# Two of the 48 paired dV stores of a cached-attention and SwiGLU backward kernel, issued in parts of 49, 49, 30 and of 49, 49, 25, 5 partitions

## The chip, the cores and the metric

The kernel runs on one core of one Trainium2 chip. The metric is the time of one execution on the device in microseconds (us).

## What is computed

The reference is one decode step of a transformer block and its gradients. Four batch rows `x` of 512 numbers pass a layer norm and attention over a key and a value cache of 32 heads of 4096 x 128 bf16 numbers for each batch row, and then a gated SwiGLU block. What is returned is the output and the gradients with respect to everything but `B_x`:

```python
def _A_ref(x, k_cache, v_cache, wq, wo):
    q = (x @ wq).reshape(B, Sq, H, Dh).transpose(0, 2, 1, 3)
    scores = jnp.einsum("bhqd,bhkd->bhqk", q, k_cache) * (Dh ** -0.5)
    p = _softmax(scores, axis=-1)
    o = jnp.einsum("bhqk,bhkd->bhqd", p, v_cache)
    return o.transpose(0, 2, 1, 3).reshape(B, Sq, H * Dh) @ wo
h = x + _A_ref(_layernorm(x), A_k_cache, A_v_cache, A_wq, A_wo)
h2 = h + _B_ref(_layernorm(h), B_w1, B_w3, B_w2)   # silu(x w1) * (x w3) @ w2
_out, _vjp = jax.vjp(_f, A_x, A_k_cache, A_v_cache, A_wq, A_wo, B_w1, B_w3, B_w2)
return (_out, *_vjp(grad_out))
```

There are 4 x 32 = 128 heads. For each, the caches K and V are 1 MB, and so are their gradients dK and dV. With one query a head, dV is an outer product of the probabilities with the head's row of dO, and dK one of dS with the row of q.

## The kernel before

All traffic between HBM and the on-chip memory goes through an `arena` of 23 slots, each 4160 bf16 columns on all 128 partitions; one head (4096 columns, 8 KB a partition) fills a slot, a pair of heads (8192 columns, 16 KB a partition) two neighbouring ones. The schedule is written out by hand: the program order on each engine is the order of the source, and all large transfers are issued by SyncE (SP), on one queue, in program order.

The forward pass loads K and V of each head (L178 and L186). The weights and V are then loaded again (V at L833 for single heads, L1280 for pairs), and the backward part stores dV (L817) and dK (L1255) of the first 32 heads one by one. The other 96 heads go as 48 pairs `t` = 0 to 47. For each pair:

- `load_pair` (L1280) brings 2 MB of V into a pair of slots, three pairs ahead of its use;
- `front_pair` transposes it on TensorE (L1298), copies it back on ScalarE (L1299) and multiplies (L1313);
- `grad_pair` is called once for dV (`out_3`, from `more_V`) and once for dK (`out_2`, from the loop over `t`). It takes a pair of slots (`Slot2`, the one that was given back longest ago), VectorE writes the outer product into it (`outer_pair`, L1379, 128 x 8192), and SP stores it (L1389): one DMA of 128 rows of 16 KB. `give()` hands the slots on; the next work that writes them waits until the store has landed.

```python
def two_heads(ap, t):
    b, h = t % B, H0 + t // B * 2
    return ap[b, h:h + 2].rearrange("h (p j) d -> (h p) (j d)", p=P // 2)
```

So a pair's 128 rows are 128 pieces of 16 KB that lie one after the other in HBM. `lead_V` lets the dV stores run ahead of the dK stores of the same pair by a few pairs, fewer towards the end. Between these, `side(s)` stores the gradients of the weights (L1072, L1119, L1135, L1146). The last eleven transfers of the program are stores of pairs (L1389).

SP has 530 transfers to issue. The program gives them eight completion semaphores in turn, and each transfer waits, besides for its data, until the one eight places before it has landed. In this order the dV store of pair 16 is number 416 (counted from 0), that of pair 34 number 482, and the last store of all is number 529.

Of the kernel before, what the change touches and what calls it, by code (L numbers as in the profile page):

```python
# [21 lines left out]
SP = 32  # L22
NPAIR = 8
OLD = 9


@with_exitstack
def kernel(
# [22 lines left out]
    nc = tc.nc  # L51
    P = nc.NUM_PARTITIONS
# [5 lines left out]
    Dh = A_k_cache.shape[3]  # L58
# [6 lines left out]
    SJ = Sk // P  # L65
# [50 lines left out]
    def age(i):  # L116
        return given["n"] - given.get(i, -NSLOT)
# [7 lines left out]
    class Slot:  # L125
        def __init__(self, name, src=free):
            self.i = src[0]
            if part["B"] and src is free:
                lone = sorted((i for i in free if i not in part["pairs"]), key=age, reverse=True)
                self.i = lone[0] if name in SIDE or lone and age(lone[0]) >= OLD else max(free, key=age)  # L130
            src.remove(self.i)
# [76 lines left out]
    for i in range(2):  # L208
        t = fcon.tile([P, 64], BF16, name=f"onesw{i}")
# [4 lines left out]
    def ones_window(col):  # L214
# [11 lines left out]
                          in_=rowg[:, None, :, None].to_broadcast([P, 4, 8, 4]))  # L226
# [738 lines left out]
    with ExitStack() as c2:  # L965
# [306 lines left out]
# [4 lines that stand above are left out]
        def load_pair():  # L1276
            t = npv["next"]
            npv["next"] += 1
            pV[t] = Slot2()
            nc.sync.dma_start(out=pV[t].t[:, 0:2 * SJ * Dh], in_=two_heads(A_v_cache, t))  # L1280

        def load_pairs(t):
            while npv["next"] < NT and (npv["next"] <= t or len(V2s) + 2 * len(pV) < 6 and len(Slot2.choices()) > 1
                                          and -min(Slot2.choices())[0] >= OLD - 2):
                load_pair()
# [92 lines left out]
        def outer_pair(dst, col2, row):  # L1378
            nc.vector.tensor_tensor(  # L1379
                out=dst.rearrange("p (j r t) -> p j r t", r=Dh // 2, t=2),  # L1380
                in0=col2[:, :, None, :].to_broadcast([P, 2 * SJ, Dh // 2, 2]),
                in1=row.rearrange("p (r t) -> p r t", t=2)[:, None, :, :].to_broadcast([P, 2 * SJ, Dh // 2, 2]),
                op=ALU.mult,
            )

        def grad_pair(out_ap, t, col2, row):
            g_ = Slot2()
            outer_pair(g_.t[:, 0:2 * SJ * Dh], col2, row)
            nc.sync.dma_start(out=two_heads(out_ap, t), in_=g_.t[:, 0:2 * SJ * Dh])  # L1389
            g_.give()  # L1390

        O0, S0, S1, L, LP = 2, 21, 35, 5, 3
# [2 lines left out]
        def more_V(upto):  # L1395
            while gvd["n"] < min(SP, upto):
                s = gvd["n"]
                P_pairs(s)
                replicate("rdo", s - s % REP)
                grad_V(s)  # L1400
                P_pairs(s + 1)
                P_pairs(s + 2)
                gvd["n"] += 1
                if s % REP == 2 and s + 2 < SP:
                    replicate("rdo", s + 2)
                elif s % REP == 2:
                    replicate_pair("rdo", 0)
                if s >= SP - 2:
                    P2_pair(s - SP + 2)
            while gvd["t"] < NT and SP + 2 * gvd["t"] + 2 <= upto:  # L1410
                t = gvd["t"]
                P2_pair(t)
                replicate_pair("rdo", t // B)
                grad_pair(out_3, t, pP2.pop(t), reps["rdo", "p", t // B][:, t % B, :])
                P2_pair(t + 1)
                gvd["t"] += 1
                if t % B == 2:
                    replicate_pair("rdo", t // B + 1)
# [57 lines left out]
        for t in range(NT):  # L1476
            s = SP + 2 * t
            load_pairs(t + LP)
            if t % B == 2:
                replicate_pair("rq", t // B + 1)  # L1480
            if t + LP < NT:
                front_pair(t + LP, lambda: side(s))
            else:
                if t + LP == NT:
                    rows_out()
                    rows_T()
                side(s)
            more_V(s + 2 + lead_V(s))
            grad_pair(out_2, t, pdS[t // 2][:, t % 2], reps["rq", "p", t // B][:, t % B, :])
            if t % 2 == 1 and t + 1 < NT:  # L1490
                group_dS_pair((t + 1) // 2)
            side(s + 1)
# [31 lines left out]
```

## Time and profile before

| | |
|---|---|
| Time, median of 3 runs | 1697.54 us (1696.87 to 1697.6) |
| Span of the profiled execution | 1696.2 us |
| Bytes read from HBM, written to it | 422.59 MB, 282.34 MB |
| Mean rate of the 16 DMA engines | 417 GB/s |
| Busy: TensorE matmul, VectorE, ScalarE, GpSimd | 73%, 73%, 57%, 20% |
| A pair's store (2048 KB), issue to landing, median | 27.9 us |
| A pair's load (2048 KB), issue to landing, median | 32.1 us |
| Outer product of a pair on VectorE (L1379) | 4.42 us |

The only time that the profiled execution has of its own is its span, from its first instruction to its last; the median of the runs is 1.3 us above it, for what lies around the span and for the scatter between executions.

How to read it: a line of the kernel is given as L and its number; SPq is SP's queue of DMA issues. "DMA" rows give the mean busy share of the 16 DMA engines of the core, so that one engine busy alone is 0.06 of them. In a list of waits, "A <- B: us, times, longest" says how long A stood still until B released it. Each DMA is carried out by several engines, and each of them reports its own part on the DMA's semaphore: the trace has sixteen such updates for every DMA of 128 rows, with their times.

### The profile page before, as it was taken

The numbers are of one execution on the slowest core, as the hardware profiler recorded it, in microseconds if no ns is written. First come the engines' busy times: TensorE is split into PE (matmuls) and PEld (weight loads), VectorE is DVE, ScalarE is ACT, GpSimd is POOL, SyncE is SP. The second block draws the span as 40 slices with busy tenths as digits, with TensorE's granted clock in tenths as the row PEclk, the third lists the DMA queues.
The fourth block names the chain that finished last, engine by engine and source line by source line (L and its number), as shares of the span: only waits on it lengthen the run. The fifth ranks groups of instructions, "written<-read, shape, count | busy, mean of one in ns | idle before, by whom it ended". The sixth has DMA issues, their size and how long they took to land.

```text
span 1696.2 us, 37839 instructions
## 1 busy us (share of the span) xinstructions
PE 1233.4 (73%) x16228; PEld 943.4 (56%) x16228; DVE 1234.4 (73%) x1198; ACT 959.5 (57%) x1490; POOL 336.9 (20%) x583
## 2 busy tenths in 40 slices
PE   5889888888888888877876755667665666766650
PEld 4777667666677666655655544444444444444440
DVE  5989999999998997667766466575665655655683
ACT  3555544454454544677665555666665666666650
POOL 1211222222222222222231121011210102011120
PEclk8999999999999999899898689886678777676675
DMA  9999999999999999999999999999999999999995
GB/s 401 424 424 424 424 424 424 424 424 423 416 423 406 424 414 397 395 414 425 425 425 429 428 429 428 429 430 429 429 429 428 418 430 429 422 418 425 415 429 230
DMA packets 81000, 707.45 MB, mean 417 GB/s; under 512 B 8748, under 2 KB 12984, under 8 KB 15296
## 3 DMA queue, kind: packets, MB, share of 16 engines
q1 hardware_dynamic: 80416, 704.94, 99.0%
q8 instruction: 127, 2.08, 0.5%
q14 instruction: 41, 0.34, 0.0%
q0 software_dynamic: 416, 0.10, 0.0%
HBM read 422.59 MB, written 282.34 MB: 416 GB/s over the span
## 4 chain that ended last, share of the span: by engine, by line
DMA 46%; DVE 9%; PE 3%; issue 2%; ACT 1%; DVEq 0%; POOL 0%; SPq 0%; ACTq 0%
DMA out_dram<-arena 43%; DVE arena L1379 7%; DMA arena<-in_A_v_cache_dram 3%; DVE arena L806 1%; PE M_ps L472 1%; DVE arena L457 1%; PE pt_w L601 0%; ACT arena L1299 0%; ACT Pn L436 0%; DVEq L1519 0%; PE kP_ps L482 0%; DVE dPr L1326 0%; PE pt_tps L1298 0%; PE gu_ps L873 0%; PE dn_ps L904 0%
## 5 line engine op out<-in xcount | busy, mean ns | idle before, releaser
L1299 ACT COPY arena<-pt_tps 128x1024 bf16<-128x1024 bf16 x384 | 369.8, 1023 | 232.3 <-PE pt_tps L1298 231.6
L1298 PE MATMUL pt_tps<-ident_b,arena 128*128 128x128 bf16 x3072 | 308.1, 272 | 204.7 <-DMA arena<-in_A_v_cache_dram 149.4
L1298 PEld LDWEIGHTS <-arena 128*128 128x128 bf16 x3072 | 263.9, 125 | 304.2 <-DMA arena<-in_A_v_cache_dram 172.8
L1379 DVE TENSOR_TENSOR arena<-arena 128x8192 bf16<-128x8192 bf16 x48 | 212.5, 4427 | 205.1 <-DMA out_dram<-arena 202.3
L472 PE MATMUL M_ps<-arena 128*128 128x130 bf16 x4096 | 285.1, 222 | 42.9 <-DMA arena<-in_A_v_cache_dram 42.2
L457 DVE TENSOR_TENSOR arena<-arena 128x4096 bf16<-128x4096 bf16 x128 | 292.5, 2285 | 23.9 <-POOL arena L453 23.9
L472 PEld LDWEIGHTS <-arena 128*128 128x128 bf16 x4096 | 251.9, 99 | 64.0 <-DMA arena<-in_A_v_cache_dram 57.2
L1379 DVE TENSOR_TENSOR arena<-dS,arena 128x8192 bf16<-128x8192 bf16 x48 | 212.3, 4424 | 73.0 <-DMA out_dram<-arena 73.0
L364 DVE STREAM_TRANSPOSE arena<-arena 128x512 f32<-128x512 f32 (+1 forms) x321 | 250.7, 797 | 0.0
L359 ACT COPY arena<-pt_tps 128x1024 bf16<-128x1024 bf16 x128 | 129.5, 1012 | 188.9 <-PE pt_tps L358 150.5
L1376 POOL COPY arena<-arena 128x128 bf16<-128x128 bf16 x48 | 55.3, 1153 | 492.3 <-ACT arena L1353 286.3
L370 POOL TENSOR_TENSOR W<-qrep,wmask 128x128 bf16<-128x128 bf16 x128 | 120.2, 939 | 85.6 <-PE S_ps L390 70.8
L801 ACT COPY arena<-pt_tps 128x1024 bf16<-128x1024 bf16 x128 | 121.7, 1025 | 26.1 <-PE pt_tps L800 24.8
L453 POOL COPY arena<-P_all 128x64 bf16<-128x64 bf16 x128 | 32.7, 255 | 412.8 <-ACT P_all L447 409.8
L806 DVE TENSOR_TENSOR arena<-dS,arena 128x4096 bf16<-128x4096 bf16 x32 | 73.2, 2293 | 35.0 <-DMA out_dram<-arena 34.7
L800 PE MATMUL pt_tps<-ident_b,arena 128*128 128x128 bf16 x1024 | 78.5, 229 | 27.1 <-ACT arena L801 27.1
L1313 PE MATMUL dP_ps<-arena 128*32 128x512 bf16 x768 | 85.7, 484 | 7.6 <-ACT arena L1299 7.3
L800 PEld LDWEIGHTS <-arena 128*128 128x128 bf16 x1024 | 67.2, 104 | 37.5 <-issue 35.9
L447 ACT COPY P_all<-pt_P 32x64 bf16<-32x64 bf16 x256 | 52.1, 204 | 53.6 <-PE pt_P L443 51.4
L806 DVE TENSOR_TENSOR arena<-P,arena 128x4096 bf16<-128x4096 bf16 x29 | 66.4, 2295 | 19.8 <-DMA out_dram<-arena 19.8
L358 PE MATMUL pt_tps<-ident_b,arena 128*128 128x128 bf16 x1024 | 80.1, 222 | 0.0
L482 PE MATMUL kP_ps<-arena,onesw 128*32 128x512 bf16 x1024 | 79.6, 388 | 0.0
(245 smaller groups left out, 1576.5 us busy)
## 6 DMA issues: line engine op xcount, KB each, us to landing
out_dram<-arena SPq DMA_DIRECT2D x96, 2048.0 KB, 27.9
arena<-in_A_v_cache_dram SPq DMA_DIRECT2D x160, 1024.0 KB, 15.9
arena<-in_A_k_cache_dram SPq DMA_DIRECT2D x128, 1024.0 KB, 15.3
arena<-in_A_v_cache_dram SPq DMA_DIRECT2D x48, 2048.0 KB, 32.1
out_dram<-arena SPq DMA_DIRECT2D x72, 1024.0 KB, 20.2
arena<-in_A_wq_dram SPq DMA_DIRECT2D x8, 1024.0 KB, 14.4
arena<-in_B_w_dram SPq DMA_DIRECT2D x8, 896.0 KB, 15.3
out_dram<-arena SPq DMA_DIRECT2D x6, 896.0 KB, 28.4
```

The costliest lines, as they stand in the source:

```text
L359: nc.scalar.copy(out=KT[:, c * GW:(c + 1) * GW, :], in_=pt[:])
L364: nc.vector.transpose(out=KT[:, c * w_:(c + n) * w_], in_=Kn[:, c * w_:(c + n) * w_])
L370: nc.gpsimd.tensor_tensor(out=W[:, hl], in0=qrep[:, :, s:s + 1].to_broadcast([P, 4, 32]), in1=wmask[:, hl, None, :].to_broadcast([P, 4, 32 ...
L457: nc.vector.tensor_tensor(out=PK[:, :, 0:Dh].rearrange("p j (r t) -> p j r t", t=2), in0=Ks[s].heads().rearrange("p j (r t) -> p j r t", t=2),
L472: nc.tensor.matmul(hold["M"][:], lhsT=Vn[:, j, :], rhs=PK[:, j, :], start=(j == 0), stop=(j == SJ - 1))
L800: nc.tensor.transpose(pt[:, i, :], v[:, g * GW + i, :], ident_b[:])
L801: nc.scalar.copy(out=v[:, g * GW:(g + 1) * GW, :], in_=pt[:])
L806: nc.vector.tensor_tensor(out=dst.rearrange("p j (r t) -> p j r t", t=2), in0=col2[:, :, None, :].to_broadcast([P, SJ, Dh // 2, 2]), in1=r ...
L1298: nc.tensor.transpose(pt[:, i, :], v[:, g * GW + i, :], ident_b[:])
L1299: nc.scalar.copy(out=v[:, g * GW:(g + 1) * GW, :], in_=pt[:])
L1313: nc.tensor.matmul(rows["acc"][32 * c:32 * (c + 1), :], lhsT=zt[t % B][:, 32 - m:64 - m], rhs=v[:, j0:j0 + 4, :], start=(pl == 0 and u == ...
L1379: nc.vector.tensor_tensor(out=dst.rearrange("p (j r t) -> p j r t", r=Dh // 2, t=2), in0=col2[:, :, None, :].to_broadcast([P, 2 * SJ, Dh / ...
```

## The change

The stores of dV for pairs 16 and 34 are issued as several DMAs, one behind the other, over consecutive partitions: 0 to 48, 49 to 97 and 98 to 127 for pair 16; 0 to 48, 49 to 97, 98 to 122 and 123 to 127 for pair 34. Every other transfer, all stores of dK among them, stays whole. The bytes, the slots and the order of all other work stay as they are.

```diff
+CUTS = {16: (49, 98), 34: (49, 98, 123)}
...
         def grad_pair(out_ap, t, col2, row):
             g_ = Slot2()
             outer_pair(g_.t[:, 0:2 * SJ * Dh], col2, row)
-            nc.sync.dma_start(out=two_heads(out_ap, t), in_=g_.t[:, 0:2 * SJ * Dh])
+            dst, src = two_heads(out_ap, t), g_.t[:, 0:2 * SJ * Dh]
+            cuts = (0, *CUTS.get(t, ()), P) if out_ap is out_3 else (0, P)
+            for p0, p1 in zip(cuts, cuts[1:]):
+                nc.sync.dma_start(out=dst[p0:p1, :], in_=src[p0:p1, :])
             g_.give()
```

SP then issues 535 transfers instead of 530, and each of the five that come in addition takes its turn among the eight semaphores. The next outer product that reuses the slots waits for all parts.

## The prediction

> **What bounds the kernel now.** I read the page's slices first, then the chain and the waits, then the windows of the last 25 us, and last the landing times of each DMA.
>
> ```profile
> DMA  9999999999999999999999999999999999999995
> DMA 46%; DVE 9%; PE 3%; issue 2%; ACT 1%; DVEq 0%; POOL 0%; SPq 0%; ACTq 0%
> q1 hardware_dynamic: 80416, 704.94, 99.0%
> q8 instruction: 127, 2.08, 0.5%
> ```
>
> The DMA engines are busy from the first slice to the last but one, and the chain that ended last is mostly DMA. So the work of the engines decides, not TensorE or VectorE (73% each). The last slice has a 5 where the others have 9. The windows (start and end, length, busy times, clock, DMA share, GB/s) show why:
>
> ```profile
> 1660.00:1670.00 10.00, 0.00 (x0) 0.00 (x0) 6.79 (x2) 0.00 (x0) 0.00 (x0) 0.50 1.01 429
> 1670.00:1676.00 6.00, 0.00 (x0) 0.00 (x0) 0.00 (x0) 0.00 (x0) 0.00 (x0) 0.50 0.86 369
> 1678.00:1686.00 8.00, 0.00 (x0) 0.00 (x0) 0.00 (x0) 0.00 (x0) 0.00 (x0) 0.50 0.07 29
> 1686.00:1694.00 8.00, 0.00 (x0) 0.00 (x0) 0.00 (x0) 0.00 (x0) 0.00 (x0) 0.50 0.06 27
> ```
>
> All compute is over, and from about 1677 to 1694.9 the DMA share is 0.06: one engine of sixteen, at 27 GB/s. The DMA view of the window from 1678 to 1696 has 31 packets, 0.44 MB:
>
> ```profile
> DMA packets 31, 0.44 MB, mean 25 GB/s; under 512 B 4, under 2 KB 4, under 8 KB 4
> ```
>
> Four are the 4-byte updates of four DMAs, 27 are rows of 16 KB, 607 ns from start to start. One engine still has the rest of four stores to write when the others have nothing left, and the program waits for it:
>
> ```profile
> SPq L1519 <- DMA out_dram<-arena: 27.6, 2, 22.8
> SPq L1389 <- DVE arena L1379: 564.8, 91, 12.1
> DVE arena L1379 <- DMA out_dram<-arena: 76.3, 18, 7.1
> ```
>
> (The third line is VectorE's waits from 1440 to 1676: the outer products wait for slots whose stores have not landed. SP, in the second, waits for those outer products.) The sixteen updates of a DMA, sorted, tell how far the engines are apart. Span times in us, of the first seven, the next eight and the last:
>
> ```
> DMA                       first seven      next eight       last
> 416 (dV, pair 16)      1156.4..1158.0   1161.4..1163.1    1171.2
> 482 (dV, pair 34)      1454.8..1455.4   1458.9..1460.4    1475.4
> 529 (the last store)   1674.6..1674.9   1676.6..1677.6    1694.9
> ```
>
> One engine trails: 9.8 us behind the middle at pair 16, 15.7 at pair 34, some 18 at the end, where the gap stops growing because new stores need slots that it must first free. From landing 416 to 529 each engine had 508.1 us of packets (836 rows of 16 KB or their worth at 607 ns, and an update of 6 ns for each DMA); the last needed 523.7 us, a factor 1.03. It was never without work, so each row costs it 0.607 x 1.03 = 0.625 us of the end. The early seven needed 517 to 518 us, so they stood for up to 9 us, 6 of them after 1356.
>
> **The change part by part.** *The whole store* gives each engine 8 rows: 128 rows, sixteen updates. *The parts* have 49, 30, 25 and 5 rows, and no DMA of the trace has such a count. Every DMA that it does have is dealt without remainder: 128 rows as 16 x 8, GpSimd's 4-row stores as 4 x 1. Dealt so over at most 16 engines, 49 rows go as 7 x 7, 30 as 15 x 2, 25 as 5 x 5, 5 as 5 x 1. If every deal begins at the same engine, the two stores together, 16 rows an engine before, become:
>
> ```
> engines      pair 16         pair 34            sum   against 16   us at 0.607
> first five   7+7+2 = 16      7+7+5+1 = 20       36       +20         +12.1
> next two     7+7+2 = 16      7+7     = 14       30       +14          +8.5
> next eight         2                  0          2       -14          -8.5
> last one           0                  0          0       -16          -9.7
> ```
>
> Which row holds the trailing engine? The two 4-row stores by GpSimd, near 1130 and 1263 us, put their 1 KB rows on four engines. Followed packet by packet to the next update, all four, both times, are among the early seven. So the engines at which a short deal begins are early, and the trailing engine isn't one of the first four. Seven early engines fit the first seven of the deal. Of the remaining nine places, eight give -14 rows and one -16; I take 14.
>
> [...]
>
> *The trailing engine* then ends 14 x 0.625 = 8.7 us earlier, at 1686.2 (10.0 and 1684.9 with 16 rows).
>
> *The first five* are late next. From 1156.4 to 1158.0 at DMA 416 they have 508.1 + 12.1 = 520.2 us of packets: 1676.6 to 1678.2 if they never stand, 1674.9 + 12.1 = 1687.0 if they stand as often as before. The second is above 1686.2, but with 8 rows more each from pair 16 on they lose the lead that made them stand; I take a value in between, and they don't decide. If the first five were of the middle eight, they would end at 1677.6 + 12.1 = 1689.7 at worst.
>
> *Five more DMAs on SP.* An issue is 0.33 us and issues of one burst start 0.44 us apart, so 5 x 0.44 = 2.2 us on a queue that stood 564.8 us at L1389; behind it only the dK store of the same turn and a V load three pairs ahead. Cost 0, or 2.2 us if that cover were gone. The nearest row for the tail of a small DMA is GpSimd's 4 KB store, 6.6 us to land, here beside other engines' work: also 0.
>
> *The semaphores.* With three or four parts in the turn of eight, a transfer behind pair 16 waits in effect for the one six places before it, behind pair 34 five places. Stores follow each other every 4.9 us and land 27.9 us after issue, 5.7 places. By the old landings, four issues behind pair 34 would wait: 483 (a dK store, 2.6 us), 484 (a weight's store, 7.3 us), 485 (a V load, 11.5 us) and 486 (5.4 us). The 14 - 8 = 6 rows that the trailing engine has lost at pair 16 take 3.8 us off each. What remains, up to 7.7 us on a load, is hidden: the load is needed three pairs (some 45 us) later, and the trailing engine has 15 us of other rows before it. The middle engines, which took 17.7 us from its issue to its landing, may stand for 3 us, and they have 8.5 us to spare. Cost 0; up to 7.7 us if that cover were gone.
>
> [...]
>
> **Sum.** 1696.2 - 8.7 = 1687.5 us of span; the median of the runs lies 1.3 us above the profile, so 1688.8 us.
>
> **The rivals.**
> 1. *The first five end last* (0.15). The standing of the early seven doesn't shrink, or the first five are engines of the middle eight. The end is 1687.0 to 1689.7 instead of 1694.9, the time 1689.6 to 1692.3. For it: the early seven's 9 us of standing. Against it: where 4-row stores go.
> 2. *Slower: the trailing engine is among the first seven* (0.08). Each row added to it moves the end by 0.625 us from the first one on: +20 rows give 1710.0 us, +14 give 1706.3. For it: no view gives its number; against it, the 4-row stores and the group of just seven early ones.
> 3. *No change* (0.04). Rows go by partition whatever the count, each engine keeps 8 of each store, and the change doesn't move what it seems to: 1697.5 us. A deal of ceil(49/16) = 4 rows an engine belongs here too if the trailing engine is among the first twelve: 4+4+2 and 4+4+2 rows or one more, +2.5 to 3.1 us at most; further back it would gain.
> 4. *Slower by the semaphores* (0.02). SP falls so far behind at pair 34 that the trailing engine itself stands. It decides from the point where SP stalls longer than its backlog, 15.7 - 3.8 = 11.9 us, against 7.7 us above. Price: some 5 us for a slot turn, with the rows' gain lost as well: about 1702.
>
> **Chances and range.** The forecast case has 0.71, rival 1 0.15: faster by over 0.2% (3.4 us, about what a measurement of this kernel can tell from no change) 0.86, within 0.2% 0.04, slower 0.10. The range takes 16 rows and 0.5 us of scatter at the low end (1687.5 - 0.7), and rival 1's worst at the upper: 1686.8 to 1692.4. Rivals 2 to 4, 0.14, are left out.
>
> **What would show it.** Right: the parts have 7, 7, 15, 7, 7, 5 and 5 data-carrying updates that come late and the others at once; the last slices still show one or a few engines, but for about 9 us less; from the DMAs behind pair 16 on the early seven land about where the middle eight do, and the last update comes 14 rows, some 8.6 us, nearer to them. The end is shared: near it five engines are busy (a share near 0.3) close to when the trailing one ends. Wrong: the old order of early, middle and last behind pair 16 (rival 3), a last update that trails more than before (rival 2), or a DMA share under 0.95 for tens of us behind pair 34 (rival 4).

## The result and the profile after

The changed kernel takes 1725.91 us in the median of 5 runs (1723.17 to 1727.47), the kernel before 1697.54 us. The ratio is 1.0164, 95% interval 1.0152 to 1.0176: 28.4 us slower, where 8.7 us faster was forecast. The profiled execution has a span of 1723.2 us against 1696.2.

The page of the kernel after: DMA share and rate in 40 slices of 43.1 us, DMA packets, and the first line of the queues.

```profile
DMA  9999999999999999999999999999999999899995
GB/s 401 424 424 424 424 424 424 424 424 423 418 421 412 424 411 397 381 425 424 426 426 428 429 428 428 430 419 372 409 413 409 411 429 424 319 408 424 414 412 231
DMA packets 81021, 707.45 MB, mean 411 GB/s; under 512 B 8769, under 2 KB 13005, under 8 KB 15317
...
q1 hardware_dynamic: 80437, 704.94, 98.4%
```

The GB/s row of the kernel before:

```profile
GB/s 401 424 424 424 424 424 424 424 424 423 416 423 406 424 414 397 395 414 425 425 425 429 428 429 428 429 430 429 429 429 428 418 430 429 422 418 425 415 429 230
```

The rate falls to 372 in the slice of pair 16 and to 319 in that of pair 34; in the four slices behind the first it is 409 to 413, where the kernel before has 418 to 429. Yet the share of busy time is a 9 in the first of these slices and an 8 in the second: the engines are mostly occupied and move less. The same bytes are moved, and SP's queue has 80437 packets instead of 80416. The 21 more are updates: two whole stores have 2 x 16, and the parts 7 + 7 + 15 + 7 + 7 + 5 + 5 = 53, as counted on the semaphores of the trace. So they go to as many engines as the prediction assumed.

The windows around the two stores say it more closely (the DMA share and GB/s are the last two columns). First before, then after:

```profile
1155.00:1175.00 20.00, 15.88 (x129) 10.51 (x128) 14.07 (x8) 14.93 (x19) 1.60 (x2) 0.59 1.01 428
1465.00:1485.00 20.00, 12.90 (x125) 7.86 (x121) 12.00 (x8) 13.50 (x19) 2.02 (x3) 0.83 1.01 421
```

```profile
1155.00:1175.00 20.00, 11.76 (x102) 7.58 (x101) 10.41 (x7) 11.26 (x15) 0.47 (x2) 0.67 1.00 369
1465.00:1485.00 20.00, 10.15 (x94) 6.79 (x90) 13.20 (x8) 10.90 (x15) 2.96 (x1) 0.72 0.77 245
```

From 1155 to 1175 the engines are fully busy in both kernels, but at 369 GB/s instead of 428. In both, the median row of 16 KB takes 611 ns from its start to its end; from 1150 to 1190, 58 of 858 such packets start that take over 1000 ns, the longest 3069, where the kernel before has 2 of 983. At pair 34 work is missing as well: a share of 0.77. That is the sign that the prediction named for its rival 4, in which SP falls behind; the first experiments ask whether it costs time.

The end still looks as before, one engine alone, in the window of the kernel after:

```profile
1712.00:1720.00 8.00, 0.00 (x0) 0.00 (x0) 0.00 (x0) 0.00 (x0) 0.00 (x0) 0.50 0.07 29
```

In SP's waits (the stores are at L1393 now) those for other transfers to land have grown, but in many short pieces, the longest of 6.2 us. First before, then after:

```profile
SPq L1389 <- DMA out_dram<-arena: 14.7, 5, 4.6
```

```profile
SPq L1393 <- DVE arena L1380: 535.5, 84, 12.2
...
SPq L1393 <- DMA out_dram<-arena: 35.2, 10, 6.2
```

The tail did not shrink, it moved. When the last engine lands the last store, 27.3 us later than before, the engine next to it is 16.9 us ahead. The updates of each part, in the order of their times, tell who the trailing engine is (span times in us; a part has one update at its issue besides, which is left out):

```
pair 16, 49 rows   1156.9 1157.4 1157.8 1159.1 1161.4 1162.4 1175.0
pair 34, 25 rows   1479.3 1480.7 1484.7 1485.5 1500.5
pair 34,  5 rows   1481.6 1481.9 1485.3 1486.3 1501.4
```

One of the seven, and one of each five, lands about 13 to 15 us after the others, and so does one, 10 to 15 us late, in the other four parts: the trailing engine has rows in all seven. Its landings, 1175.0, 1181.2 and 1182.6 at pair 16 and 1491.4, 1496.5, 1500.5 and 1501.4 at pair 34, are as far apart as 7 and 2 rows and 7, 5 and 1 rows of 0.7 to 0.9 us. So it carries rows of the 5-row part too, and if all parts begin at the same engine, it is among the first five. By that count it got 16 rows instead of 8 at pair 16 and 20 at pair 34.

### The profile page after: what moved, and what is told of

Same layout as the page of the kernel before. It is cut to its first block, busy times and chain, and to the rows that moved or that the text cites. A ratio compares the mean times of both kernels' runs of the same rounds, so it can differ in the third digit from the quotient of the medians.

```text
span 1723.2 us, 37846 instructions
## 1 busy us (share of the span) xinstructions
PE 1239.7 (72%) x16228; PEld 953.0 (55%) x16228; DVE 1234.4 (72%) x1198; ACT 959.6 (56%) x1490; POOL 336.3 (20%) x583
## 3 DMA queue, kind: packets, MB, share of 16 engines
q1 hardware_dynamic: 80437, 704.94, 98.4%
## 4 chain that ended last, share of the span: by engine, by line
DMA 39%; DVE 9%; PE 6%; ACT 5%; issue 2%; POOL 1%; DVEq 0%; SPq 0%; ACTq 0%
DMA out_dram<-arena 39%; DVE arena L1380 7%; ACT arena L802 4%; PE pt_tps L801 1%; DVE arena L807 1%; PE dq_ps L1001 1%; PE dP_ps L1229 1%; PE M_ps L473 1%; PE pt_w L602 1%; DVE arena L458 1%; PE pt_wo L611 1%; POOL zd L1194 0%; ACT Pn L437 0%; DVE dPr L1327 0%; DVEq L1523 0%
## 5 line engine op out<-in xcount | busy, mean ns | idle before, releaser
L1299 PE MATMUL pt_tps<-ident_b,arena 128*128 128x128 bf16 x3072 | 310.6, 273 | 229.0 <-DMA arena<-in_A_v_cache_dram 176.8
L1299 PEld LDWEIGHTS <-arena 128*128 128x128 bf16 x3072 | 266.7, 126 | 328.9 <-DMA arena<-in_A_v_cache_dram 199.4
L473 PEld LDWEIGHTS <-arena 128*128 128x128 bf16 x4096 | 252.4, 99 | 63.4 <-DMA arena<-in_A_v_cache_dram 56.7
L1377 POOL COPY arena<-arena 128x128 bf16<-128x128 bf16 x48 | 48.4, 1010 | 519.1 <-ACT arena L1354 277.8
L801 PE MATMUL pt_tps<-ident_b,arena 128*128 128x128 bf16 x1024 | 84.3, 240 | 24.1 <-ACT arena L802 24.1
L801 PEld LDWEIGHTS <-arena 128*128 128x128 bf16 x1024 | 72.9, 110 | 34.7 <-issue 33.3
L359 PE MATMUL pt_tps<-ident_b,arena 128*128 128x128 bf16 x1024 | 80.5, 223 | 0.0
```

The lines of the kernel that those rows point to most:

```text
L473: nc.tensor.matmul(hold["M"][:], lhsT=Vn[:, j, :], rhs=PK[:, j, :], start=(j == 0), stop=(j == SJ - 1))
L801: nc.tensor.transpose(pt[:, i, :], v[:, g * GW + i, :], ident_b[:])
L1299: nc.tensor.transpose(pt[:, i, :], v[:, g * GW + i, :], ident_b[:])
```

## The experiments

Theory A: the end moves by the rows that the trailing engine gains, 8 + 12 of them at 0.625 us, 12.5 us in all. Theory B: besides, rows carried by another engine than in a whole store are slow and slow others. Theory C: the additional DMAs hold SP up through the eight semaphores. A alone leaves 16 of the 28.4 us unexplained, so the first four runs ask where these come from. Rows on an engine are counted as in the prediction's table. Each ratio is against the kernel before, measured beside it on the same chip.

### As many parts, cut by columns

```diff
-CUTS = {16: (49, 98), 34: (49, 98, 123)}
+CUTS = {16: (2752, 5504), 34: (2048, 4096, 6144)}
...
-            cuts = (0, *CUTS.get(t, ()), P) if out_ap is out_3 else (0, P)
-            for p0, p1 in zip(cuts, cuts[1:]):
-                nc.sync.dma_start(out=dst[p0:p1, :], in_=src[p0:p1, :])
+            W = 2 * SJ * Dh
+            cuts = (0, *CUTS.get(t, ()), W) if out_ap is out_3 else (0, W)
+            for c0, c1 in zip(cuts, cuts[1:]):
+                nc.sync.dma_start(out=dst[:, c0:c1], in_=src[:, c0:c1])
```

> The same two stores are cut into as many DMAs as in the change (three and four), but by columns: each part has all 128 partitions, so each engine carries the rows that it carries in a whole store, and as many bytes. Theory A (the end moves by the rows that the trailing engine gains, 0.625 us each): 0, 1697.5 us. Theory B (besides, a row costs more when it is carried by another engine than in a whole store): 0 as well, 1697.5. Theory C (the five additional DMAs use up the turn of eight semaphores and SP falls behind): a good part of the change's 28 us stays; what the 20 rows that A counts (8 + 12, 12.5 us) leave over is about 15 us, so 1705 to 1713.

Measured: 1698.94 us, ratio 1.0008 (0.9999 to 1.0017), 0 to 2.9 us. Theory C falls: the five DMAs with their issues and semaphores cost next to nothing. The windows of this kernel at pair 16 and at pair 34:

```profile
1155.00:1175.00 20.00, 14.23 (x131) 9.86 (x130) 13.47 (x8) 15.35 (x20) 2.53 (x2) 0.76 1.01 418
1465.00:1485.00 20.00, 12.77 (x126) 7.92 (x124) 12.67 (x9) 13.59 (x19) 2.46 (x3) 0.84 0.97 376
```

At pair 16 it has almost the old rate. At pair 34 it has not: 376 GB/s instead of 421. But the trailing engine lands at most 2.6 us later there than in the kernel before, and the last store 1.5 us later: what is lost there stays small for the engine that sets the end.

### Two halves of 64 partitions

```diff
-CUTS = {16: (49, 98), 34: (49, 98, 123)}
+CUTS = {16: (64,), 34: (64,)}
```

> The two stores are cut into two halves of 64 partitions: 4 rows an engine in each half, 8 together, as in the whole store, but over other partitions than those that the engine has in a whole store. Theory A (rows of the trailing engine): 0, 1697.5 us. Theory B (rows carried by another engine than in a whole store slow themselves and the others): slower though no engine has more to do, by some 3 to 10 us, 1701 to 1707, with packets of 16 KB over 1000 ns around both stores. Theory C (semaphores): two additional DMAs, near 0.

Measured: 1708.67 us (1704.51 to 1709.46), ratio 1.0064 (1.0047 to 1.0081): 8 to 14 us slower, though by the deal (64 rows as 16 x 4) no engine has a row more. Theory A can't make this, theory B does, and at the median by more than its estimate of 3 to 10. The window:

```profile
1155.00:1175.00 20.00, 11.64 (x106) 7.64 (x104) 10.41 (x7) 11.14 (x15) 0.48 (x2) 0.68 1.00 356
```

Fully busy at 356 GB/s, and 68 of 889 rows from 1150 to 1190 take over 1000 ns.

### One store at a time

```diff
-CUTS = {16: (49, 98), 34: (49, 98, 123)}
+CUTS = {16: (49, 98)}
```

> Only the store of pair 16 is cut (49, 49, 30). Theory A: the trailing engine has 8 rows more, +5.0 us, 1702.5. Theory B: 5.0 for the rows and about 7 to 10 us of slowed packets, as the trace of the change shows at this place: 1709.5 to 1713. Theory C: two additional DMAs, a stall of a few us that is made up later, 1697.5 to 1700.

Measured: 1715.7 us, ratio 1.0104 (1.0089 to 1.0119), +17.9 us. Neither A nor C reaches it, and it is more than B's estimate.

```diff
-CUTS = {16: (49, 98), 34: (49, 98, 123)}
+CUTS = {34: (49, 98, 123)}
```

> Only the store of pair 34 is cut (49, 49, 25, 5). Theory A: the trailing engine is one of the first five, 12 rows more, +7.5 us, 1705. Theory B: 7.5 for the rows and 3 to 5 us of slowed packets, 1708 to 1710. Theory C: most of the change's loss is here, where four parts take half of the turn of eight: over 1712.

Measured: 1711.57 us, ratio 1.0081 (1.0066 to 1.0096), +13.8 us: above B's 1710 and near C's 1712, had the cut by columns left C standing. The two stores together would make 31.7 us; the change has 28.4.

### The place of the trailing engine

```diff
-CUTS = {16: (49, 98), 34: (49, 98, 123)}
+CUTS = {16: (112, 113, 115, 118, 122, 127)}
```

> The dV store of pair 16 is cut into 112, 1, 2, 3, 4, 5 and 1 partitions, pair 34 stays whole. If a DMA of k rows goes to the first k engines, the smallest k whose landing trails by some 10 us tells the place of the trailing engine. Theory A and B agree on the place: k = 4 does not trail if the four engines of GpSimd's 4-row stores are the first four, and k = 5 does, since the 25-row and 5-row parts of the change trailed. Time: A expects 7+1+1 rows or so instead of 8 on the trailing engine, +0.6 us, 1698; B some 5 us of slowed packets more, as in the halves of 64, 1702 to 1706.

Measured: one time, 1702.29 us beside 1698.15 of before, too little to tell A from B. The updates of the small parts (span times in us):

```
1 row    1157.5
2 rows   1158.1 1158.6
3 rows   1158.4 1158.9 1159.2
4 rows   1158.0 1159.0 1159.7 1159.8
5 rows   1160.9 1161.1 1161.1 1161.1 1175.4
```

Four rows land together, of five rows one lands 14 us late. So, if a deal of k rows goes to the first k engines, the first four are early ones and the fifth is the one that trails.

This run bears on theory C too. SP stands 13.3 us for stores to land here, the DMA share falls to 0.49 from 1155 to 1175 (196 GB/s), and yet the trailing engine goes from 4.1 us late at the load before pair 16 to only 5.3 us two transfers behind it. It has a backlog, and SP's stalls are hidden behind that.

### Leaving the two stores out

```diff
-CUTS = {16: (49, 98), 34: (49, 98, 123)}
+CUTS = {16: (), 34: ()}
...
-            cuts = (0, *CUTS.get(t, ()), P) if out_ap is out_3 else (0, P)
+            cuts = (0,) if out_ap is out_3 and t in CUTS else (0, P)
```

> The two dV stores (pairs 16 and 34) are left out, so these parts of the output are not written. No row goes another way. Every engine has 16 rows less, the trailing one 16 x 0.625 = 10.0 us. If the trailing engine's rows set the end at that price (A and B), the time is 1697.5 - 10.0 = 1687.5 (1686 to 1689). If the stores are hidden and the change's loss is only of slowed packets, near 1697.

Measured: 1688.62 us, ratio 0.9947 (0.993 to 0.9963), -9.5 us against the forecast -10.0. The price of a row on the trailing engine, when no row changes its engine, agrees: 9.5 / 16 = 0.59 us, with an interval of 6.3 to 11.9 us for the 16 rows.

### The same cuts in the last store

```diff
-CUTS = {16: (49, 98), 34: (49, 98, 123)}
+CUTS = {47: (49, 98)}
...
-            cuts = (0, *CUTS.get(t, ()), P) if out_ap is out_3 else (0, P)
+            cuts = (0, *CUTS.get(t, ()), P) if out_ap is out_2 else (0, P)
```

> Only the very last store (dK of pair 47) is cut into 49, 49 and 30 partitions; the other engines are done when the trailing one comes to it. Theory A: 8 rows more on the trailing engine at the 607 ns of an engine alone, +4.9 us, 1702.4. Theory B: the same, for no other engine's rows are there to be in the way: 1702 to 1704, against +18 us for the same cut at pair 16. If a row costs more on another engine even without other traffic: 1706 or more.

Measured: 1705.81 us, ratio 1.0045 (1.003 to 1.006), +7.7 us: above what both theories said. With `CUTS = {47: (64,)}` in the same place:

> Only the very last store (dK of pair 47) is cut into two halves of 64 partitions. Every engine keeps 8 rows, over other partitions. Theory A: 0, 1697.5. Theory B: 0 to 1 us, 1697.5 to 1698.5, since the trailing engine writes its last rows alone, against about 5 us for each of the two cuts of this kind at pairs 16 and 34.

Measured: 1701.2 us, ratio 1.0016 (1.0007 to 1.0026), +3.0 us, against 0 to 1. The reason shows in the landings of the trailing engine. In both kernels it lands the whole stores just before the cut one some 3 us late (with 49, 49, 30 two of them come 6.2 and 6.7 us after their predecessors instead of 4.8), while the other engines, which are 17 us ahead, write the parts. So the trailing engine isn't alone when it counts: it is slowed in whole stores of its own. With 49, 49, 30 it is 2.9 us late two stores before the cut one, 3.2 one store before it, and another 5.0 for its 8 rows: 8.2 us in the profiled execution, 7.7 in the median. By its time this run would also fit the third case of its expectation, a row that is dearer even without other traffic. The landings rule that out: once alone, the trailing engine writes its 16 rows of the three parts in 9.8 us, 0.61 us each. So a row of a part is not slow by itself; in these runs it was slow only while other engines were at work too.

### Rows taken off the trailing engine

With the fifth engine taken as the one that trails, 124 and 4 partitions should keep it out altogether: by the deal of the change, where 49 rows went to 7 engines and 25 to 5, 124 rows would go as 4 x 31. That is an estimate from those counts; the four landings below agree with it.

```diff
-CUTS = {16: (49, 98), 34: (49, 98, 123)}
+CUTS = {47: (124,)}
...
-            cuts = (0, *CUTS.get(t, ()), P) if out_ap is out_3 else (0, P)
+            cuts = (0, *CUTS.get(t, ()), P) if out_ap is out_2 else (0, P)
```

> Only the very last store (dK of pair 47) is cut, into 124 and 4 partitions. By the deal that the runs have shown so far, 124 rows go to 4 engines, 31 each, and 4 rows to the same 4; the trailing engine is the fifth and gets none. Theory A (its rows alone decide): it ends 8 rows earlier, 4.9 us; the first four write 32 rows of 607 ns after about 1669.8, till 1689.3 to 1690, so the end is near 1690.4 and the time 1693. Theory B (rows carried by another engine than in a whole store are in the way of the engine whose partitions they are): the first four slow the trailing engine on its earlier stores by about 3 us, as the other engines did in the same place with 49, 49, 30 and with the halves; time 1695 to 1697. If it is the way to the partitions that is slow and not the engine: no gain, 1697.5 or more.

Measured: 1701.44 us, ratio 1.002 (1.0011 to 1.0029), +3.1 us: no gain where A has 1693, and above B's 1697; the third case of the expectation, no gain, is the one whose time fits. That the way to the partitions is what is slow, the run does not show. The trailing engine, now without the last store, ends at 1691.9 instead of 1694.9, so it did lose work, but its own last whole store took it 7.3 us instead of 4.8. And the first four bring the 124 rows home at 1693.6 to 1697.6. From their landing of the store before at about 1669.2 that is 24.4 to 28.4 us for 31 rows, 0.79 to 0.92 us a row instead of 0.607, with only the trailing engine at work beside them (their 4-row part lands last, at 1698.2):

```profile
1672.00:1690.00 18.00, 0.00 (x0) 0.00 (x0) 0.00 (x0) 0.00 (x0) 0.00 (x0) 0.50 0.32 97
```

A share of 0.32 is five engines; 97 GB/s are 19.4 for each, where one alone had 27 in the kernel before.

The same cut at pair 16 (`CUTS = {16: (124,)}`, for dV):

> The dV store of pair 16 is cut into 124 and 4 partitions, all on the first four engines, 32 rows each instead of 8; the trailing engine, the fifth, has none of the store's rows instead of 8. Theory A: the trailing engine ends 5.0 us earlier; the first four are 24 rows (14.6 us) later, which takes them from 4 us ahead of the middle to 10 us behind it, as far as the trailing engine then is: 1693 to 1697.5. Theory B: slower all the same, since 120 of the 128 rows are carried by another engine: some 5 us on the trailing engine, as for the halves at this place, and the four late engines hold slots: 1697.5 to 1705.

Measured: 1709.9 us, ratio 1.0073 (1.006 to 1.0087), +11.5 us, well above B's range. The first four land the 124 rows at 1173.5, 1179.0, 1184.6 and 1187.1. From their landing of the load before at about 1152 that is 0.69 to 1.13 us a row. From then on the slowest of these four is the one that lands last.

### 120 and 8 partitions

```diff
-CUTS = {16: (49, 98), 34: (49, 98, 123)}
+CUTS = {16: (120,), 34: (120,)}
```

> The dV stores of pairs 16 and 34 are cut into 120 and 8 partitions: 15 engines with 8 rows each, then 8 engines with one each; the trailing engine gets 9 rows instead of 8 twice. Theory A: 2 rows, +1.25 us, 1698.8. Theory B depends on how a whole store is dealt: if engine n carries the partitions 8n to 8n+7, the part of 120 keeps every row at its engine and only 8 rows move: 1698.8 to 1701. If a whole store is dealt in another pattern, most rows move, as in the halves: 1703 to 1709.

Measured: 1711.26 us, ratio 1.0073 (1.0058 to 1.0088), +12.9 us. By the deal that is one row more on the trailing engine for each store, and the loss is about as large as with the halves (10.9 us). The window:

```profile
1155.00:1175.00 20.00, 11.15 (x101) 8.01 (x100) 10.41 (x7) 10.97 (x14) 0.43 (x2) 0.67 1.00 369
```

Fully busy again, at 369 GB/s. The expectation had 1698.8 to 1701 us if engine n carries the partitions 8n to 8n+7 of a whole store, since this cut would then leave all but 8 rows at their engines, and 1703 to 1709 if a whole store is dealt in another pattern. The time speaks against the first; the pattern itself no run here shows.

### The same deal at other addresses

Is it which engine reads which partitions, or the HBM addresses?

```diff
-CUTS = {16: (49, 98), 34: (49, 98, 123)}
+CUTS = {16: (), 34: ()}
...
-            cuts = (0, *CUTS.get(t, ()), P) if out_ap is out_3 else (0, P)
+            if out_ap is out_3 and t in CUTS:
+                b_, h_ = t % B, H0 + t // B * 2
+                far = out_ap[b_, h_:h_ + 4].rearrange("h (p j) d -> (h p) (j d)", p=P // 2)
+                dst = far[49:49 + P, :]
+            cuts = (0, P)
```

> The dV stores of pairs 16 and 34 stay whole, 128 partitions each, but are written 49 rows (49 x 16 KB) further on in HBM; the first 49 rows of each of these two pairs are therefore not written. Each engine keeps its partitions and its 8 rows, and only the HBM addresses that an engine writes are others than in a whole store. If what slows the parts lies on the side of HBM (an engine that writes addresses that another one writes in a whole store): slower by some 10 us, as for the halves and for 120 and 8. If it lies on the side of the partitions (theory B): 0, 1698, and the rows of 16 KB keep their 611 ns around both stores. Theory A: 0.

Measured: 1697.74 us, ratio 0.9999 (0.999 to 1.0009). Other addresses alone cost nothing. The window has the old rate:

```profile
1155.00:1175.00 20.00, 13.02 (x124) 8.68 (x122) 13.84 (x8) 14.22 (x19) 3.61 (x2) 0.76 1.00 428
```

Of the two, what is left is which engine reads which partitions. Why that costs time no run here shows.

### The loss, added up

How much later the trailing engine lands than in the kernel before, in the profiled executions, by the place in SP's order:

```
                      number  before    change  cols   halves  16 only  34 only
well before pair 16      410  1141.3     -0.2   +0.5    +1.3     +1.2     +1.7
load before pair 16      415  1166.2     +4.4   +0.5    +5.4     +5.3     +1.7
dV of pair 16            416  1171.2    +11.4   +0.6    +5.4    +12.0     +1.7
24 places on             440  1282.0    +14.4   +0.5    +5.9    +14.1     +1.7
before pair 34           481  1470.3    +16.6   +0.2    +7.4    +15.2     +3.7
dV of pair 34            482  1475.4    +25.9   +0.3    +7.4    +15.2    +12.3
the last store           529  1694.9    +27.3   +1.5    +6.6    +17.5    +15.5
```

For the change: 4.6 us come before the trailing engine has reached the first part, in its whole stores and its load, while others write the parts. 7.0 come in the parts, 5.0 of them for 8 rows. 3.7 follow up to 1418 and 1.5 just before pair 34. There the parts make 9.3, of which 7.5 are for 12 rows, and 1.4 come after. Rows: 12.5. Rows and stores slowed at the two places: 4.6 + 2.0 + 1.5 + 1.8 = 9.9. The rest, 5.1 us in steps of 1 to 2 over the following tens of us, has no run of its own. The column of the halves shows the slowing alone, 4.1 us at pair 16. Its profiled execution is 6.5 us longer than that of before, while its median is 10.9 us longer; the sizes here are those of one execution.

## Why the prediction was wrong

- **What bounds the kernel** was right: one engine that trails, its rows at about 0.6 us each. Leaving out 16 of them gave 9.5 us of the forecast 10.0.
- **The deal** was right: 7, 7, 15, 7, 7, 5 and 5 updates, and the trailing engine lands last in every part, as when all begin at the same engine.
- **The place of the trailing engine** was the first step that failed. The 4-row transfers (the second of them, near 1263 us, is a load and not a store, which changes nothing in the argument) exclude the first four engines, and they are indeed early ones. But "Seven early engines fit the first seven of the deal" was a count and no observation. The fifth trails (of 5 rows one landed 14 us late, of 4 none), so not all of the first seven are early, and -14 rows became +20. As a term of the sum: -8.7 us became +12.5. This was rival 2, with 0.08. The 4-row transfers had left twelve places open, three of them in the first seven: 0.25 would have been fair.
- **The price of a row** was the second. The prediction took 0.607 to 0.625 us for every row, on whichever engine, and rival 2 with it: 1710.0 us instead of 1725.9. The sum has no term for slowed rows. Beside other work a row of a part cost 0.69 to 1.13 us (124 rows at pair 16), and whole transfers were slowed at the same time (4.6 us on the trailing engine before its first part in the change). The halves show this alone, 8 to 14 us without, by the deal, a row more for anyone. With the right place and the old price the forecast would still have missed by 16 us.
- **Five more DMAs and the semaphores**, costed at 0: right, 0 to 2.9 us by the cut by columns. The sign of rival 4, a DMA share under 0.95, did come at pair 34 (0.77), but its mechanism did not: the trailing engine landed its 20 rows there one part after the other in 14.4 us and never waited for SP. The missing work is then that of engines which are ahead. Rival 4 is out.
- **The first five end last** (rival 1): they did, but only in that the trailing engine is one of them; its four neighbours land the last store 16.9 us earlier or more.
- **The DMA share as a sign** can't tell a full-speed row from a slowed one: from 1155 to 1175 it is 1.00 at 369 GB/s in the change and 1.01 at 428 GB/s before. GB/s beside it can.

The two errors point the same way and add up: the place turned -8.7 us into +12.5. Of the 16 us beyond that, 9.9 in the profiled execution are rows and stores slowed at the two places, and some 5 have no run of their own.

## What to carry to other kernels

In this kernel a DMA over fewer partitions than its neighbours was not only a smaller DMA: 49 rows went to 7 engines instead of 128 to 16. The DMA engines bound the kernel, and beside other work rows of a part took up to 1.13 us instead of 0.607 (124 rows at pair 16), while whole transfers were slowed too (4.6 us before the first part in the change). Where a transfer has to be cut, try the cut by columns first: it cost 0 to 2.9 us here. When one engine trails, find out which one (parts of 1 to 5 rows showed it in one run here) before moving work away from it. Read the DMA share and GB/s together: here a share of 1.00 at 369 instead of 428 GB/s went with 58 rows over 1000 ns instead of 2.

## What was not expected of the hardware

- Around stores that were cut by partitions rows got slow: beside a median of 611 ns, 58 of 858 rows take over 1000 ns and up to 3069 at pair 16 of the change, and with 124 and 4 partitions in the last store five engines with a share of 0.32 move 97 GB/s instead of five times 27. With 49, 49, 30 in the last store, the trailing engine alone takes 0.61 us for a row of a part.
- The engine that trails, the fifth, does so with the same bytes as all others: 523.7 us for 508.1 us of packets from pair 16 to the end. Why it is 3% slower no run here tells.
- Taking the last store off the trailing engine gained nothing: it ended 3.0 us earlier, and the four that took its rows later than it had (1698.2 against 1694.9).
